# Attention and Fourier filter in one kernel: helper copies of the queries and keys issued one segment later, the last segment's v rows in buffers of their own, and the first feature loads placed behind a stack of queries

## The chip, the cores and the metric

The kernel runs on one core of a Trainium2 chip. The time is the device time of one execution in microseconds (us); three runs of the kernel before took 716.06 to 720.59, median 717.18. One further execution was recorded by the hardware profiler: it took 717.81 us, and the span from its first to its last instruction is 716.1 us. All instruction times below come from that execution and count from the start of the span. TensorE is called PE, VectorE DVE, ScalarE ACT, GpSimd POOL and SyncE SP; SP does no arithmetic, it issues DMAs, in the order of the program, and waits.

## The reference

Two independent computations, whose results stand side by side in the output.

```python
# A: causal attention in 4 segments of 512 rows, 32 heads of 18, with a memory carried between segments
q,k,v = x@wq, x@wk, x@wv
for s in range(4):
    p = softmax(qs @ ks.T * scale + mask);  a_dot = p @ vs
    num = phi(qs) @ M;  den = phi(qs) @ z + 1e-6          # phi(t) = t+1 if t>0 else exp(t)
    outs.append(g * num/den + (1-g) * a_dot)              # g = sigmoid(beta)
    M = M + phi(ks).T @ vs;  z = z + phi(ks).sum(rows)
a = concat(outs) @ wo
# B: a filter in the frequency domain
b = irfft2(rfft2(x) * (w_r + 1j*w_i))
```

x of A is 2048 x 576, x of B 2048 x 576, everything in float32.

## The kernel before, in words

The order of the work is written out by hand. Python generators emit the instructions; each engine then runs its own instructions in the order in which they were emitted, and an instruction waits for the data, and for the buffers, that it needs. The tiles come from rotating pools: a tile with `bufs=2` can be allocated again once the work on its allocation before the last one is over, DMAs that read it included.

There are four stages.

1. **Forward transform of B** (0 to about 75 us).
2. **Projections of A** (about 75 to 277 us, `projections`, L557). For each of the four segments g come nine units `qk_unit` (L472), each 14 products of 128 x 512 for 128 columns of the queries or keys, and four units `v_unit` (L509), each 14 products of 288 columns for either half of 128 rows of v. A queries-and-keys unit splits its result into three bf16 parts and stores them in DRAM as `qkD` (L499). A unit of v copies its result into a tile `vt` (two buffers; POOL fills its constant columns, L519 and L520, ACT copies the rest, L522) and SP stores it in `vD` (L523). For the segments 0 to 2 the features phi(k) are collected in a tile `pk` (one buffer of 128 x 4 x 576) and multiplied with `vt` for the memory (L529); the last segment needs no memory and doesn't allocate `pk`. The units of B's middle part run on DVE and ACT in between.
3. **Inverse transform of B** (about 277 to 355 us, `inverse`, L287) in 16 units u. A unit multiplies its spectrum with a table `civ` (L300, 18 products), splits the result into tiles `T` (ACT L330 and L337, DVE L332 and L338), and two units later multiplies those with a table `itab` (L311, 14 products); ACT and DVE form the output `yout` (L316 to L319, three buffers) and SP stores it (L320). Between its steps runs `prologue` (L965), which does the first ten score units `s1` (L677) of the attention, three steps each, and pops one or two DMAs per step from a list: the loads for the next stacks.
4. **Attention** (355 us to the end, `attention`, L987), a loop over t=0..132 with one unit of the 128 (segment, head) pairs per trip. Trip t does the scores `s1(t+10)` for the row maxima and `s2(t)` (L720) for the exponentials, and the product with v (`pv`, L749) of earlier trips. The heads are worked in 16 stacks n of eight. The stack's queries `Qs` (three buffers) and keys `Ks` (four) are loaded by seven DMAs each (`stack_dmas`, L655): six of 128 KB from `qkD` and one of 96 KB from a second DRAM tensor `reD`. At the first trip of stack n the loop queues the queries of stack n+2, the keys of stack n+3 and the v rows of stack n+2, and pops two per trip; `s1(8(n+2))`, in trip 8n+6, is the first to read the new queries.

The helper tensor `reD` holds rows 16 and 17 of every head (a head has 18 rows, a stack's DMA takes 16). It is filled per segment by `rest` (L547): twelve copies `reD<-qkD` from DRAM to DRAM, 64 rows of 1 KB each, six for the queries and six for the keys. Before the change all twelve are issued on SP in the segment that produced them, six ahead of unit 11 and six ahead of unit 12, that is among the units of v.

`pq_load` (L799) loads one of five tiles of the features phi(q) of a segment: four of 126 x 512 float32 (252 KB) and one of 72 x 512 (144 KB). Those of segment 1 are loaded in the trips 16 to 20, one each, ahead of the stack load of the trip; they are first read by `den` (L805), which is set in at trip 34.

Of the kernel before, what the change touches and what calls it, by code (L numbers as in the profile page):

```python
# [5 lines left out]
F32=mybir.dt.float32; F32R=mybir.dt.float32r  # L6
# [387 lines left out]
class ATT:  # L394
# [114 lines left out]
    def v_unit(s,g,tb,tp,pp):  # L509
        nc=s.nc  # L510
        P=[]
        for hf in range(2):
            ps=pp.tile([128,288],F32,name="pjv",tag="pj")
            yield from s.passes(ps,g,"wv",slice(288*hf,288*hf+288),slice(128*tb,128*tb+128),True)
            P.append(ps)
            yield
        vt=tp.tile([128,622],F32,name="vt")
        vv=vt[:,:608].rearrange("p (h c) -> p h c",c=19)
        nc.gpsimd.memset(vv[:,:,18:19],1.0)  # L519
        nc.gpsimd.memset(vt[:,608:],0.0)  # L520
        for hf in range(2):
            nc.scalar.copy(vv[:,16*hf:16*hf+16,:18],P[hf].rearrange("p (h c) -> p h c",c=18))  # L522
        nc.sync.dma_start(s.vD[g][tb],vt)  # L523
        if g==3: return
        for _ in range(3): yield
        if tb==0: s.pm=[pp.tile([126,3,7,19],F32,name=f"pm{i}",tag="pm") for i in range(2)]
        for t in range(5):
            w=7 if t<4 else 4; r=18*w
            nc.tensor.matmul(s.pm[t//3][:r,t%3,:w].rearrange("p h c -> p (h c)"),s.pk[:,tb,126*t:126*t+r],vt[:,133*t:133*t+19*w],  # L529
                start=tb==0 and t%3==0,stop=tb==3,skip_group_check=True)  # L530
        if tb<3: return
        yield
        n=g+1
        for t in range(5):
            w=7 if t<4 else 4; r=18*w
            m=tp.tile([126,7,19],F32,name="mm")
            nc.vector.tensor_tensor(m[:r,:w],s.pm[t//3][:r,t%3,:w],s.bm[:r,:w],op=OP.mult)
            z=s.zst[n][:r,t,:w]
            for o,h0,h1,c0,c1 in ((0,0,7,0,18),) if t<4 else ((0,0,2,0,18),(36,2,3,0,12),(48,1,2,6,18),(60,2,4,0,18)):
                k=(h1-h0)*(c1-c0)  # L540
                M,N=[x[:r,t,o:o+k].rearrange("p (h c) -> p h c",c=c1-c0) if x is not None else None for x in (s.Mst[n],s.Mst[g])]
                x=m[:r,h0:h1,c0:c1]
                if n==1: nc.gpsimd.tensor_copy(M,x)
                else: nc.gpsimd.tensor_tensor(M,x,N,op=OP.add)
            if n==1: nc.gpsimd.tensor_copy(z,m[:r,:w,18])
            else: nc.gpsimd.tensor_tensor(z,m[:r,:w,18],s.zst[g][:r,t,:w],op=OP.add)
# [10 lines left out]
    def projections(s,xp,tp,pp,wv,pace,hook):  # L557

        live=[]
        s.nid=wv.tile([128,128],BF,name="nid"); s.nc.scalar.activation(s.nid,s.ident,AF.Copy,scale=-1.0)  # L560
        lw=s.load_w("wv",576,wv,xp,288,"xl",4)
        def advance():
            for l in list(live):
                try: next(l)
                except StopIteration: live.remove(l)
        tot=pace.left-12
        for g in range(4):
            if g<3: xq=[s.xprep(g+1,t,(xp,s.x0)[g%2],xp,[128,512],"xst",2) for t in range(5)]
            rest=s.rest(g)
            for i in range(13):  # L570
                for _ in range(6 if i>10 else 0): rest.pop(0)()
                u=s.qk_unit(g,i,tp,pp) if i<9 else s.v_unit(g,i-9,tp,pp)
                if i==4 and g<3: s.pk=tp.tile([128,4,576],F32,name="pk",bufs=1)
                next(u)
                hook(g,i)
                next(lw,None); next(lw,None)
                if g<3 and i in (4,6,8,10,12): next(xq[(i-4)//2])
                if g<3 and i in (1,3,5,7,9): next(xq[(i-1)//2])
                w=tot/(36-18*.3+12*2.7+3*2.0+.2)*((2.7 if g<3 else 2.0 if i<12 else .2) if i>8 else .7 if s.third(g,i) else 1.0)
                advance()  # L580
                pace.take(w*.7)
                advance()
                next(u)
                pace.take(w*.3)
                live.append(u)
        while live: advance()

    def att_setup(s,cp):
# [376 lines left out]
    def prologue(s):  # L965

        nc,io=s.nc,s.io
        yield
        s.masks()
        s.load_v(0)  # L970
        q=s.stack_dmas(1,0)+s.stack_dmas(1,1)+s.stack_dmas(2,0)+s.stack_dmas(2,1)+[lambda: s.load_v(1)]+s.stack_dmas(3,1)
        for i in range(2): yield
        i=0
        for t in range(10):
            for _ in s.s1(t):
                for _ in range(1+(i%5==0)):
                    if q: q.pop(0)()
                i+=1
                yield
            if 2<=t<6: nc.gpsimd.dma_start(s.Ks[t-2][108:110].rearrange("p h c -> p (h c)"),io["neg1"])  # L980
            if t in (3,7): m=s.mpath(t//4); next(m)
            if t in (4,8): next(m); next(m,None)
        assert not q
    def homes(s):

        for n,t,b in (("oh",F32R,5),("ol",F32R,5),("am",F32,5),("pq",F32,5),("ux",F32,3)): s.tp.tile([126 if n in ("am","pq") else 128,512],t,name=n,bufs=b)
    def attention(s,tp,ps):  # L987
        nc=s.nc; s.tp,s.ps,s.psm,s.mtag=tp,ps,s.ps1,"s1"
        s.homes()
        def steps(gen,i):  # L990
            for _ in range(i):
                try: next(gen)
                except StopIteration: return
        m=None
        q=[]
# [12 lines left out]
        for t in range(133):  # L1008
            k,hh=divmod(t,4); n,qd=divmod(k,2); g=k//8
            if t==3: nc.gpsimd.memset(s.cap,3.0e38)  # L1010
            if t==4: nc.gpsimd.affine_select(out=s.cap,in_=s.cap,pattern=[[1,128]],compare_op=OP.is_ge,fill=0.0,base=0,channel_multiplier=-1)
            if hh==0 and qd==0:
                if 0<n<14: q+=s.stack_dmas(n+2,0)
                if 0<n<13: q+=s.stack_dmas(n+3,1)
                if n+2<16: q.append(lambda n=n: s.load_v(n+2))
            st=t%32
            if 16<=t<21: s.pq_load(1,t-16)
            if t==34: bg.insert(0,s.den(1,lane))
            if st==8 and g>0:
                def ln(g=g):  # L1020
                    r=s.recip(s.rD[g-1],s.rrD[g-1],s.g1,False,"rr",2)
                    for i in range(8):
                        next(r)
                        if 2<i<6: s.ux_load(g-1,i-3)
                        yield
                    yield from r
                    bg.append(s.mixed(g))
                    if g<3: bg.append(s.between(g,lane))
                lane.append(ln())
            if t==124: lane.append(s.recip(s.rD[3],s.rrD[3],s.g1,False,"rr"))  # L1030
            if 125<=t<128: s.ux_load(3,t-125)
            a=s.s1(t+10) if t+10<128 else iter(())
            b=s.s2(t) if t<128 else iter(())
            if q: q.pop(0)()
            if qu: qu.pop(0)()
            if hh==(0 if k>29 else 3) and m is not None: steps(m,1)
            steps(a,1)
            steps(b,1)
            r=(t-5)%4
            if r%2: run_bg(1)  # L1040
            steps(a,1)
            steps(b,1)
            if 5<=t<129: s.pv((t-5)//4,(t-5)%4)
            if t==129:
                for j in range(4): s.pv(31,j)
                s.pv_out(31)
                u=s.u_dmas(15)
                rb=s.recip(s.rD[3],s.rrD[0],s.g1,False,"re")
                qu+=[u[0],lambda: next(rb)]+u[1:]
            steps(a,1)  # L1050
            steps(b,1)
            s.free=not bg and t<116
            if hh==(3 if k==29 else 2) and m is not None: steps(m,1)
            if hh==1 and k+2<32: m=s.mpath(k+2); next(m)
            if 7<=t<131 and t%4==3:
                s.pv_out((t-7)//4)
                if t%8==3:
                    u=s.u_dmas((t-11)//8)
                    if t<120: s.later(1,lambda u=u: qu.extend(u))
                    else: qu+=u  # L1060
            for l in list(lane):
                try: next(l)
                except StopIteration: lane.remove(l)
            if q: q.pop(0)()
            if qu: qu.pop(0)()
            run_bg((.3,1,.5,1)[r])
            s.due(t)
# [3 lines left out]
        i=0  # L1071
# [28 lines left out]
        for u in range(8):  # L1100
            tb,hf=divmod(u,2); s.last_proj(u,4,None if u>2 else 1)
# [105 lines left out]
```

## Time and profile before

| | us |
|---|---|
| median of three runs | 717.18 |
| profiled execution | 717.81 |
| its span | 716.1 |
| PE busy | 674.7 (94%) |
| DVE busy | 558.0 (78%) |
| ACT busy | 443.5 (62%) |
| POOL busy | 215.1 (30%) |

A matmul is shown from its start to its modelled end, and matmuls overlap, so a PE that is busy all the time is not at its peak; what counts is where it stands idle and what ended that. A row of the timeline gives start, duration, engine, line, operation, output and inputs, shapes and count, and in brackets the idle time before it with what released it. In a row of stretches stand the length, the busy time of each engine with its count of instructions, the granted share of the PE clock, the mean busy share of the 16 DMA engines (over 1 where packets overlap) and GB/s.

### The profile page before, as it was taken

Reading aid. Unit: us, or ns where it says so; the run is one execution under the profiler, and the core shown is the slowest. Engines: PE = TensorE matmul, PEld = TensorE weight load, DVE = VectorE, ACT = ScalarE, POOL = GpSimd, SP = SyncE. Lnnn points to the kernel's source line nnn. Section 1 sums busy time; section 2 is a strip of 40 time slices with the busy share of each in tenths; the row PEclk is TensorE's granted clock in tenths of the full one; section 3 lists DMA queues with packets and bytes.
Section 4 is the critical chain, followed back from the end, with each engine's and each line's share of the span. In section 5 each row is a group of like instructions: output and inputs, shape, how many; then the busy total and the mean of one; then the engine's idle time right before and its main releaser. Section 6 shows DMA issues by size and latency. Waiting matters only on the chain.

```text
span 716.1 us, 14217 instructions
## 1 busy us (share of the span) xinstructions
PE 674.7 (94%) x4829; PEld 496.4 (69%) x4829; DVE 558.0 (78%) x1237; ACT 443.5 (62%) x999; POOL 215.1 (30%) x422
## 2 busy tenths in 40 slices
PE   4999999999999998999989699998999999999997
PEld 4999779889779788999844354444566445564677
DVE  5999999899989886698588587987656876568353
ACT  3667795583584562444378477776766777667741
POOL 2110000100200211365156553543424564245210
PEclk9999999999999999899999899999999999999999
DMA  9877446555664778999639987979768988552232
GB/s 339 269 230 205 149 141 210 198 186 167 207 204 139 215 219 278 196 230 224 169 91 190 167 161 146 188 151 167 134 148 166 166 156 156 130 139 67 87 101 81
DMA packets 89321, 124.73 MB, mean 174 GB/s; under 512 B 13994, under 2 KB 56600, under 8 KB 89112
## 3 DMA queue, kind: packets, MB, share of 16 engines
q1 hardware_dynamic: 82656, 107.78, 61.4%
q0 software_dynamic: 6592, 16.04, 8.9%
q8 instruction: 38, 0.62, 0.4%
q14 instruction: 35, 0.29, 0.2%
HBM read 85.45 MB, written 41.39 MB: 177 GB/s over the span
## 4 chain that ended last, share of the span: by engine, by line
PE 65%; DVE 11%; DMA 10%; ACT 8%; issue 4%; POOL 1%; SPq 0%; ACTq 0%; DVEq 0%; POOLq 0%
PE pv L758 9%; PE pj L469 7%; PE po L919 6%; PE pjv L469 5%; PE s L684 5%; PE i L300 4%; PE i L311 4%; PE s L692 4%; PE s L728 3%; PE s L732 2%; DMA vD<-vt 2%; PE po L951 2%; DMA Qs<-qkD 2%; PE pm L529 2%; DMA xin<-xb 2%
## 5 line engine op out<-in xcount | busy, mean ns | idle before, releaser
L688 DVE CUSTOM_DVE_ANT_0 junk<-s,mask 128x512 bf16<-128x512 f32 (+1 forms) x256 | 141.5, 553 | 54.1 <-PE s L684 42.1
L694 DVE TENSOR_REDUCE mx<-s 128x4 f32<-128x512 f32 x128 | 87.8, 686 | 23.7 <-PE s L693 22.4
L729 ACT ACTIVATE P<-s 128x512 f32<-128x512 f32 x128 | 77.2, 603 | 26.5 <-PE s L728 24.7
L734 ACT ACTIVATE P<-s 128x512 f32<-128x512 f32 x128 | 76.9, 601 | 8.7 <-PE s L733 5.0
L758 PE MATMUL pv<-P,vs 128*32 128x512 f32 (+3 forms) x1024 | 82.1, 439 | 0.0
L738 ACT ACTIVATE P<-s 128x256 f32<-128x256 f32 x128 | 49.4, 386 | 47.8 <-PE s L737 47.7
L741 POOL TENSOR_SCALAR_AFFINE_SELECT P<-P 128x512 f32<-128x512 f32 x116 | 69.6, 640 | 4.1 <-ACT P L729 3.4
L758 PEld LDWEIGHTS pv<-P,vs 128*32 128x32 f32 x1024 | 26.7, 109 | 45.0 <-issue 41.5
L469 PE MATMUL pj<-x,wqkh 128*128 128x512 f32 x162 | 55.9, 406 | 0.0
L519 POOL MEMSET vt<- 128x32 f32 x16 | 2.4, 162 | 155.2 <-PE pm L529 110.8
L210 DVE TENSOR_TENSOR t<-Z 128x580 f32<-128x580 f32 x64 | 46.4, 755 | 0.1
L210 DVE TENSOR_TENSOR Z<-t 128x580 f32<-128x580 f32 x64 | 45.8, 753 | 0.0
L300 PE MATMUL i<-civ,Y 128*128 128x256 f32 (+1 forms) x288 | 39.7, 293 | 3.3 <-DVE T L332 3.3
L684 PE MATMUL s<-Ks,Qs 108*128 108x512 bf16 (+1 forms) x128 | 42.1, 329 | 0.0
L493 ACT CAST sp<-pj 128x512 bf16<-128x512 f32 x36 | 21.1, 585 | 31.9 <-DVE pj L489 31.9
L142 PE MATMUL f<-ftab,eh 128*128 128x290 f32 (+1 forms) x160 | 31.0, 312 | 10.0 <-DMA ftab<-ftab 10.0
L300 PEld LDWEIGHTS i<-civ,Y 128*128 128x128 f32 (+1 forms) x288 | 37.5, 189 | 3.5 <-DVE T L332 3.5
L311 PE MATMUL i<-itab,T 128*128 128x290 f32 (+1 forms) x224 | 37.1, 316 | 0.1
L469 PEld LDWEIGHTS pj<-x,wqkh 128*128 128x128 f32 x162 | 30.4, 188 | 8.7 <-issue 2.0
L469 PE MATMUL pj<-xh,wqkl 128*128 128x512 f32 x90 | 35.6, 395 | 0.0
L469 PE MATMUL pj<-x,wqkl 128*128 128x512 f32 x90 | 35.6, 395 | 0.0
L469 PE MATMUL pj<-xh,wqkh 128*128 128x512 f32 x90 | 35.5, 395 | 0.0
(227 smaller groups left out, 1833.0 us busy)
## 6 DMA issues: line engine op xcount, KB each, us to landing
qkD<-sp SPq DMA_DIRECT2D x36, 384.0 KB
Ks<-qkD SPq DMA_DIRECT2D x72, 128.0 KB
x<-qkD SPq DMA_DIRECT2D x60, 128.0 KB
Qs<-qkD SPq DMA_DIRECT2D x60, 128.0 KB
xin<-xb SPq DMA_DIRECT2D x16, 384.0 KB
cfw<-cfw POOLq DMA_DIRECT2D x16, 384.0 KB, 4.4
civ<-civ POOLq DMA_DIRECT2D x16, 384.0 KB, 6.3
vs<-vD SPq DMA_DIRECT2D x16, 330.0 KB
```

The source lines that it names most:

```text
L210: v.tensor_tensor(o,a,b,op=op)
L300: nc.tensor.matmul(p[:m,k],Y[i][:,q,c*128:c*128+m],cc[:,hl,o:o+256],start=n==0,stop=n==5)
L311: nc.tensor.matmul(p,x,t,start=n==0,stop=n==6)
L469: s.nc.tensor.matmul(out,a,b,start=i==0,stop=i==len(L)-1)
L684: nc.tensor.matmul(out,Q[:108,h,128*i:128*i+128],K[:108,h,:128*(i+1)],start=True,stop=True)
L688: nc.vector.tensor_tensor_reduce(out=junk[:,:w],in0=src,in1=s.mask[:,512-w:],scale=1.0,scalar=-3.0e38, op0=OP.add,op1=OP.max,accum_out=s.m ...
L694: nc.vector.tensor_reduce(out=s.mx[k][:,hh],in_=pa.rearrange("p (b c) -> p b c",c=128),axis=mybir.AxisListType.X,op=OP.max)
L729: nc.scalar.activation(P[0][:,hh],p0,AF.Exp,scale=SC)
L734: nc.scalar.activation(P[1][:,hh],p1,AF.Exp,scale=SC)
L738: nc.scalar.activation(P[2][:,hh],p2,AF.Exp,scale=SC)
L741: if k<29: nc.gpsimd.affine_select(out=x,in_=x,pattern=pat+[[1,128]],compare_op=OP.is_ge,fill=0.0,base=0,channel_multiplier=-1)
L758: nc.tensor.matmul(s.pvt[32*hh:32*hh+32,128*j:],vt[:,j,19*h:19*h+32],mv[0][:,hh,mv[1]],start=j==0,stop=j==2,skip_group_check=True)
```

## The change

Three edits, all in the order of work and in buffers; the arithmetic stays.

- **Copies.** `s.left=s.rest(g)` keeps the twelve copies of segment g until the next segment, where two each are issued ahead of the units 2 to 7. The last segment's twelve are issued in the prologue, one at every second step, behind the stack loads of that step.
- **Buffers of v.** In the last segment the units 0 to 2 of v write slices of a fresh `pk` tile, 622 columns each, and only unit 3 takes a `vt` buffer.
- **Features.** The five loads of segment 1's phi(q) go from the trips 16 to 20 to the trips 19 to 23.

```diff
@@ v_unit
-        vt=tp.tile([128,622],F32,name="vt")
+        if g==3 and tb==0: s.pk=tp.tile([128,4,576],F32,name="pk",bufs=1).rearrange("p a b -> p (a b)")
+        vt=s.pk[:,622*tb:622*tb+622] if g==3 and tb<3 else tp.tile([128,622],F32,name="vt")
@@ projections
-            rest=s.rest(g)
             for i in range(13):
-                for _ in range(6 if i>10 else 0): rest.pop(0)()
+                if g>0 and 1<i<8:
+                    for _ in range(2): s.left.pop(0)()
...
                 live.append(u)
+            s.left=s.rest(g)
         while live: advance()
@@ prologue
                 for _ in range(1+(i%5==0)):
                     if q: q.pop(0)()
+                if i%2 and s.left: s.left.pop(0)()
                 i+=1
                 yield
...
-        assert not q
+        assert not q and not s.left
@@ attention
-            if 16<=t<21: s.pq_load(1,t-16)
+            if 19<=t<24: s.pq_load(1,t-19)
```

## The prediction

> **What bounds the kernel now.** I read the page first, then the stretches of each stage, then PE's waits in them, and then the chain of waits and the rows of each engine around the two places where PE stands still.
>
> ```profile
> PE 674.7 (94%) x4829; PEld 496.4 (69%) x4829; DVE 558.0 (78%) x1237; ACT 443.5 (62%) x999; POOL 215.1 (30%) x422
> ```
>
> PE is busy 94% of the span; what can be won lies in the idle 41 us and in work done at a lower clock. The stretches, in the columns explained above:
>
> ```profile
> 75.00:128.00 53.00, 51.64 (x295) 43.59 (x294) 51.01 (x83) 37.36 (x83) 0.34 (x4) 1.00 0.53 169
> 286.00:300.00 14.00, 14.00 (x95) 13.53 (x93) 7.66 (x17) 6.41 (x16) 4.87 (x7) 0.81 0.82 187
> 300.00:350.00 50.00, 50.00 (x396) 47.72 (x395) 42.31 (x101) 22.48 (x55) 26.28 (x39) 1.00 1.18 226
> 386.00:412.00 26.00, 19.77 (x160) 9.25 (x159) 15.43 (x47) 14.09 (x34) 15.07 (x22) 0.87 0.92 180
> ```
>
> The inverse transform (300 to 350) is full on PE and full on the DMA engines at once, 1.18. Behind 286, PE has a clock of only 0.81. In 386 to 412 it is idle for 6.2 us and has 0.87, with the DMA engines at 0.92. The longest waits of PE in 75 to 277, 277 to 300 and 360 to 716 are:
>
> ```profile
> PE pj L497 <- ACT sp L493: 3.0, 4, 0.9
> PE i L300 <- DVE T L332: 3.3, 1, 3.3
> PE s L692 <- DMA pq<-pqD: 5.8, 1, 5.8
> ```
>
> The projections lose 3.0 us in four waits, none of them on v or on the copies: what the change does to the segments 0 to 2 is off PE's path. The other two waits are the places the change touches.
>
> **The first place: end of the projections.** The chain of waits and the rows of PE, ACT, DVE and SP:
>
> ```profile
> 266.93 8.40 DMA vD<-vt
> 275.40 4.42 DMA vD<-vt
> 281.19 2.88 DMA vD<-vt
> 289.22 2.82 PE i L311 x14
> 292.04 2.15 PE i L300 x18
> 341.44 1.90 PE i L311 x14
> ```
>
> ```profile
> 277.28 4.43 PE L300 MATMUL i<-civ,Y 128*128 128x256 f32 x36
> 285.01 4.21 PE L300 MATMUL i<-civ,Y 128*128 128x256 f32 x18 [3.30 <-DVE T L332]
> 275.42 0.71 ACT L522 COPY vt<-pjv 128x288 f32<-128x288 f32 x2 [4.05 <-DMA vD<-vt]
> 279.92 0.70 ACT L522 COPY vt<-pjv 128x288 f32<-128x288 f32 x2 [3.79 <-DMA vD<-vt]
> 280.50 0.60 ACT L330 CAST T<-i 128x512 fp32r<-128x512 f32 x1
> 281.24 1.04 ACT L284 CAST Y<-Z 128x512 fp32r<-128x512 f32 x2
> 282.19 0.58 ACT L330 CAST T<-i 128x512 fp32r<-128x512 f32 x1
> 284.27 0.69 DVE L332 TENSOR_TENSOR T<-i,T 128x512 fp32r<-128x512 f32 x1 [1.98 <-POOL Y L285]
> 270.99 3.80 SPq L555 DMA_DIRECT2D reD<-qkD  x6
> 277.20 3.88 SPq L555 DMA_DIRECT2D reD<-qkD  x6
> ```
>
> Two groups of six copies hold SP for 3.80 and 3.88 us, each ahead of a store of v (275.40 and 281.19). ACT waits 4.05 and 3.79 us for `vt` buffers that those stores empty, so the splits of the inverse's first units (280.50, 282.19) come late. DVE's split at 284.27 starts 0.2 us after the third store lands (281.19+2.88=284.07); POOL, named there, is not what the chain follows. I read it as a T tile that lies where that `vt` buffer was. PE, done with 36 products at 281.71, waits to 285.01, and then does 18 products in 4.21 us and 14 in 2.82, for which it later takes 2.15 and 1.90.
>
> *After.* The three slices need no store to land; unit 3 takes a buffer that segment 2 left. The one wait that is added, for the old `pk`, ends with segment 2's sums, which PE does before any product of segment 3's v. ACT's copies follow their products, which end as the 36 begin, and its first split follows 12 of the 36 products: 277.28+12x0.123=278.8 (0.123 is 4.43/36). It lasts 0.60, the small split after it about 0.4 (an estimate: fewer columns), the casts 1.04: ACT is free at 281.0, just when the second unit's first twelve products (the 30th of 36, 280.97) are done. Split to 281.7, DVE 0.69 to 282.4: PE goes on at 282.5 instead of 285.01, 2.5 us sooner. The last store of v, issued at about 278.2, behind ACT's 0.70, with nothing ahead of it on SP, lands by 281.1 at the 2.88 of its neighbour, ahead of DVE. POOL's fills of `vt`, queued behind the same stores, go early too; its next work follows ACT's casts. PE's idle time is then 0.8 us, no more than its waits of 0.9 in the projections, whose stretches show a clock of 1.00, so the slow products go too: 4.21-2.15=2.06 and 2.82-1.90=0.92. Sum: 2.5+2.06+0.92=**5.5 us**. What is late next is PE itself; the stretch from 300 on has not a tenth idle. Bounds: 2.5 if the clock falls all the same, 6.3 if no gap is left.
>
> **The copies, where they go.** In segments 1 to 3: twelve issues each at 3.80/6=0.63 us, two per unit, ahead of that unit's stores on SP. They wait for nothing (their source landed a segment ago), and the DMA engines have room there (0.53). They delay stores by up to 1.3 us; that reaches PE only through buffers two or three units deep. Zero, and if that cover were gone 1.3 us less per unit.
>
> In the prologue they are not free: twelve DMAs of 64 KB are 768 KB, at 226 GB/s (221 KB/us) **3.5 us** of DMA time in a stage that has none left. SP, late, then holds back the stores of `yout`:
>
> ```profile
> 337.89 0.36 SPq L320 DMA_DIRECT2D yb<-yout  x1
> 347.46 0.46 DVE L318 TENSOR_TENSOR yout<-E,i 128x290 f32<-128x290 f32 x1 [0.89 <-ACT E L316]
> 391.47 8.38 DMA Qs<-qkD
> ```
>
> Three buffers: the store issued at 337.89 must land before DVE's 347.46, 9.57 us later; transfers that queue take 8.4 (391.47 and, above, 266.93). So 1.2 us are to spare, and 3.5-1.2=2.3 us reach DVE. DVE has 15% idle time there and PE reads two units behind it, so I put 0.5 us on PE; bounds 0 and 2.3.
>
> **The second place: trip 22.** SP's rows, a wait of SP in 386 to 412, and PE's rows:
>
> ```profile
> 389.59 0.49 SPq L803 DMA_DIRECT2D pq<-pqD  x1
> ...
> 394.64 2.27 SPq L668 DMA_DIRECT2D Qs<-qkD  x2
> 397.06 0.33 SPq L803 DMA_DIRECT2D pq<-pqD  x1
> 397.83 0.30 SPq L668 DMA_DIRECT2D Qs<-reD  x1
> SPq L668 <- DMA vs<-vD: 1.3, 1, 1.3
> ```
>
> ```profile
> 394.69 1.28 PE L758 MATMUL pv<-P,vs 128*32 128x384 f32 x16
> 398.55 1.30 PE L758 MATMUL pv<-P,vs 128*32 128x512 f32 x16
> 399.90 0.27 PE L737 MATMUL s<-Qs,Ks 110*128 110x256 bf16 x1
> 405.99 0.58 PE L692 MATMUL s<-x,Qs 108*128 108x384 bf16 x2 [5.82 <-DMA pq<-pqD]
> 410.45 0.93 PE L758 MATMUL pv<-P,vs 128*32 128x384 f32 x8
> 423.90 0.38 PE L692 MATMUL s<-Ks,Qs 108*128 108x384 bf16 x2
> ```
>
> Two trips take 398.55-394.69=3.86 us; the pair with the wait takes 410.45-398.55=11.90, so 8.0 are lost: 5.8 idle, 2.0 in products at a lower clock (0.58 for L692, else 0.38). PE's wait is for stack 4's queries, whose seventh load is issued at 397.83. Four feature loads (first 389.59, fourth 397.06) go ahead of it through the same queue; SP is the only queue that they are moved in, past the six loads of Qs. SP's wait says that the v load before them landed at 394.6. From there to 405.9 came 4x252+6x128+96=1872 KB, 166 KB/us; the stretch has 180 GB/s (176 KB/us). I take 170.
>
> *After*, one feature load is ahead: 252+768+96=1116 KB, 6.6 us: the queries land at 401.2. PE wants them at 400.2 (399.90+0.27). **1.0 us** of wait instead of 5.8.
>
> But the DMA engines were full, and the loads moved back now stand ahead of stack 5's queries, which trip 30 wants. Before, trip 30 began at 423.90. After, it is due eight trips, 4x3.9=15.6 us, past 401.2: 416.8. Behind 401.2 must land stack 5's keys 864, features 3x252+144=900, v 330 (128x4x165 floats), four stores of U 288 (36 rows of 2 KB each) and stack 5's queries 864: 3246 KB, 19.1 us: **420.3**. So PE waits there for 3.5 us, and the gain at trip 30 is 423.9-420.3=3.6 of the 8.0. Bounds, by 158 (5% under what was measured) and 176 KB/us: 1.7 and 4.5. Both waits over 3 us (3.30 and 5.82) were followed by a lowered clock that cost 2 to 3 us; I charge 2.0 here. **1.6 us** stay. Past trip 30 no features are left in the way: stack 6 has a full 15.6 us.
>
> **The sum.** 5.5-0.5+1.6=6.6 us off the profiled 717.81: 711.2. The median of the runs is 0.6 below that execution, so 710.6.
>
> **The rivals.**
> *The clock holds at trip 30* (the wait is 3.5 us, hardly longer than the 3.30 that lost it): 2.0 more, 708.6. [...]
> *No second wait*: transfers speed up when the features no longer stand in front, and all 8.0 stay: 717.2-13.0=704.2. Against it: 0.92 to 1.18 wherever loads queue.
> *The copies hold up the inverse by the whole 2.3 us and a little clock*: 713.
> *The slices are not kept apart*: if the program waits per tile, each v unit waits for the store before it, 4 us as now, and the first 5.5 are gone: 716. Against: `Qs` and `Ks` of stack 0 also share one tile and are loaded and read independently.
> *Slower: the twelve copies cost a turn in the queue instead of bytes.* The prologue's transfers take 8.4 us with eight under way, 1.05 us a turn. Twelve turns are 12.6 us; less 1.2 to spare and about 2 of PE's distance to DVE, PE stands 9.4 us: 717.2-5.5+9.4-1.6=719.5. It decides from (5.5+1.6+3.2)/12=0.86 us a copy; 768 KB at the measured rate give 0.29. Nothing shows a small copy costing a whole turn: SP issued six in 3.80.
>
> **How the numbers follow.** Forecast 0.42, clock holds 0.22, no second wait 0.10, inverse held up 0.12, slices 0.08, slower 0.06. The likeliest is 710.6. The range 705.0 to 715.5 leaves out half of "no second wait", the slices and the slower case, and takes in both rates of the second place and the 2.3 of the copies. One per cent, about what a measurement of this kernel tells from no change, is 7.2 us: faster means below 710.0. That is a third of the forecast, most of "clock holds" and all of "no second wait": 0.42. Within: 0.54. Slower by over 1% (above 724.4) needs the slower case to be worse than priced: 0.04.
>
> **What would show it.** First place: no wait of ACT for vD at 270 to 280, PE's wait for DVE L332 under 1.5 us, clock 1.00 behind it. Prologue: DVE L318 waiting for yb, or not. Second place: PE's wait at trip 22 about 1 us, a new wait of L692 for a Qs load eight trips later of 2 to 5 us, and whether the clock drops there. Wrong would be: a wait of over 3 us inside the inverse, or no wait at trip 30.

## The result and the profile after

| | before | after |
|---|---|---|
| median, same chip, us | 718.22 (714.70 to 722.11, 13 runs) | 713.49 (708.35 to 715.77, 13 runs) |
| profiled execution, us | 717.81 | 712.57 |
| its span, us | 716.1 | 710.8 |

The ratio of after to before is 0.9923, with a 95% interval of 0.9899 to 0.9948: 0.8% faster, 4.7 us by the medians and 5.2 us by the profiled executions. That is within 1%, and between the two bounds of the predicted range; the forecast was 710.6.

The page's line of busy times, and three of the stretches that were shown of before (286 to 300, 300 to 350, 386 to 412), in the changed kernel:

```profile
PE 673.3 (95%) x4829; PEld 494.5 (70%) x4829; DVE 558.2 (79%) x1237; ACT 444.2 (62%) x999; POOL 215.2 (30%) x422
```

```profile
286.00:300.00 14.00, 14.00 (x112) 13.22 (x111) 11.75 (x27) 6.96 (x18) 7.50 (x10) 1.00 1.03 204
300.00:350.00 50.00, 49.95 (x390) 47.51 (x390) 39.62 (x95) 21.17 (x52) 23.27 (x36) 1.00 0.97 228
386.00:412.00 26.00, 23.21 (x195) 11.25 (x188) 18.24 (x56) 16.99 (x43) 15.37 (x24) 0.93 1.01 173
```

Behind 286 the clock is 1.00 where it was 0.81, and 112 matmuls fit where 95 did. In 386 to 412 PE is idle for 2.8 us instead of 6.2, at 0.93 instead of 0.87. Lines of the attention have moved down by two: L692 is now L694, L668 is L670.

The first place, in the rows of PE, ACT and SP of the changed kernel (start, duration, and in brackets the idle time before the row):

```profile
282.33 2.39 PE L300 MATMUL i<-civ,Y 128*128 128x256 f32 x18 [0.76 <-DVE T L332]
284.56 2.05 PE L311 MATMUL i<-itab,T 128*128 128x290 f32 x14
...
341.78 2.31 PE L300 MATMUL i<-civ,Y 128*128 128x256 f32 x18
```

```profile
279.20 0.59 ACT L330 CAST T<-i 128x512 fp32r<-128x512 f32 x1 [1.44 <-DMA vD<-pk]
```

```profile
277.82 0.32 SPq L524 DMA_DIRECT2D vD<-vt  x1
```

PE stands 0.76 us where it stood 3.30, and the 18 and 14 products behind it take 2.39 and 2.05 us where they took 4.21 and 2.82. The last store of v is issued at 277.82; before, the last two went out one behind the other from 281.19 on. At the end of the inverse PE's last 18 products with `civ` start at 341.78; before, the same row stood at

```profile
347.20 2.31 PE L300 MATMUL i<-civ,Y 128*128 128x256 f32 x18
```

so the whole stage came 5.42 us earlier. One wait is new: ACT's first split stands 1.44 us for the store out of a slice of `pk`.

The attention, in the rows of PE around its three longest waits between 355 and 716:

```profile
394.50 0.27 PE L739 MATMUL s<-Qs,Ks 110*128 110x256 bf16 x1
397.45 0.38 PE L694 MATMUL s<-x,Qs 108*128 108x384 bf16 x2 [2.68 <-DMA Ks<-qkD]
...
416.94 0.38 PE L694 MATMUL s<-Ks,Qs 108*128 108x384 bf16 x2 [2.00 <-DMA Ks<-qkD]
...
492.70 0.39 PE L694 MATMUL s<-Ks,x 108*128 108x384 bf16 x2 [1.66 <-DMA x<-reD]
498.39 0.38 PE L694 MATMUL s<-Ks,x 108*128 108x384 bf16 x2
```

The rows of L694 are the trips 22, 30, 62 and 64. (The transfer named as a releaser is the one that landed last by then; what the first two rows read is `Qs`.) Before, they began at 405.99, 423.90 (both shown), and

```profile
499.49 0.39 PE L692 MATMUL s<-Ks,x 108*128 108x384 bf16 x2 [1.49 <-DMA x<-reD]
...
503.93 0.38 PE L692 MATMUL s<-Ks,x 108*128 108x384 bf16 x2
```

The gain over before is thus 5.42 us at the end of the inverse, 8.54 at trip 22 (405.99-397.45), 6.96 at trip 30, 6.79 at trip 62, 5.54 at trip 64, and 5.3 at the end of the span. The wait at trip 22 fell from 5.82 to 2.68, one of 2.00 appeared at trip 30, and 1.25 us were lost between trip 62 and trip 64, where the wait is hardly longer than before (1.66 against 1.49).

The granted clock says what happened there. From 20 us on, but for the last 2 us, it falls in the trace of before to 0.50 at 284.37 and 403.84, 35 times 3.413 us apart, each time for 6.83 us; in the trace of after at 398.37 and 493.94, 28 times 3.413 us apart, each time for 3.41. So I cut the time into steps of 3.41 us that end at these instants. In the changed kernel, two steps at trip 22, two at trip 30, two at trip 62 (length, PE busy, ..., and the granted clock third from the end):

```profile
394.96:398.36 3.40, 0.91 (x6) 0.58 (x7) 0.57 (x4) 0.49 (x3) 1.77 (x3) 1.00 0.98 164
398.37:401.78 3.41, 3.41 (x21) 1.62 (x22) 2.77 (x8) 2.55 (x6) 1.25 (x2) 0.50 0.88 197
...
415.44:418.84 3.40, 1.90 (x14) 1.27 (x15) 1.30 (x3) 1.16 (x4) 0.42 (x2) 1.00 0.92 133
418.86:422.26 3.40, 3.40 (x32) 1.72 (x31) 2.94 (x9) 2.48 (x7) 2.78 (x5) 1.00 0.65 169
490.53:493.94 3.41, 1.75 (x19) 0.93 (x12) 1.21 (x5) 0.95 (x3) 0.42 (x2) 1.00 0.93 180
493.95:497.35 3.40, 3.40 (x19) 1.32 (x20) 2.88 (x8) 3.34 (x9) 1.45 (x2) 0.50 0.66 167
```

PE was idle for 2.49 us of the first step (73%), and the clock of the next is half. At trip 30 it was idle for 1.50 us of a step (44%), and the clock held. At trip 62 it was idle for 1.66 us of 3.41 (49%), and the next step ran at half clock.

### The profile page after: what moved, and what is told of

Its sections match the earlier page's. It is cut to its first block, busy times and chain, and to the rows that moved or that the text cites. A ratio compares the mean times of both kernels' runs of the same rounds, so it can differ in the third digit from the quotient of the medians.

```text
span 710.8 us, 14215 instructions
## 1 busy us (share of the span) xinstructions
PE 673.3 (95%) x4829; PEld 494.5 (70%) x4829; DVE 558.2 (79%) x1237; ACT 444.2 (62%) x999; POOL 215.2 (30%) x422
## 4 chain that ended last, share of the span: by engine, by line
PE 55%; DVE 12%; ACT 7%; DMA 7%; issue 4%; POOL 1%; SPq 0%; DVEq 0%; ACTq 0%; POOLq 0%
PE pv L760 9%; PE po L921 6%; PE s L686 5%; PE pjv L469 5%; PE i L300 4%; PE i L311 4%; PE s L694 4%; PE pj L469 3%; PE s L730 3%; PE s L734 2%; PE po L953 2%; DVE pj L489 2%; DMA Ks<-qkD 2%; PE s L695 2%; DVE junk L690 2%
## 5 line engine op out<-in xcount | busy, mean ns | idle before, releaser
L300 PE MATMUL i<-civ,Y 128*128 128x256 f32 (+1 forms) x288 | 37.9, 284 | 0.8 <-DVE T L332 0.8
L300 PEld LDWEIGHTS i<-civ,Y 128*128 128x128 f32 (+1 forms) x288 | 35.8, 181 | 1.0 <-DVE T L332 1.0
```

Of the source, the lines that this page charges most:

```text
L300: nc.tensor.matmul(p[:m,k],Y[i][:,q,c*128:c*128+m],cc[:,hl,o:o+256],start=n==0,stop=n==5)
```

## The experiments

The theory behind them: the copies among the units of v and the v buffers together made the first wait, and the features are worth the rest. The rivals: one of the two alone made it; the features give nothing in sum; the copies cost time where they went. Each was run beside the kernel before on the same chip: the first four rows on one chip, where the kernel before had a median of 719.16 us, the last four on another, with 719.25. Rows of different chips are compared by their ratios. The diffs are against the changed kernel, except where the text says otherwise.

| kernel | median, us (runs) | ratio to before, 95% interval |
|---|---|---|
| features back at the trips 16 to 20 | 714.55 (9) | 0.9926, 0.9897 to 0.9955 |
| copies back among the units of v | 719.65 (10) | 1.0003, 0.9972 to 1.0035 |
| two `vt` buffers as before | 712.00 (4) | 0.9891, 0.9847 to 0.9936 |
| features at the trips 0 to 4 | 706.86 (4) | 0.9822, 0.9779 to 0.9866 |
| prologue's copies issued twice | 712.98 (10) | 0.9917, 0.9890 to 0.9945 |
| features at 0 to 4 and two `vt` buffers | 707.50 (6) | 0.9839, 0.9808 to 0.9871 |
| copies moved for the last segment only | 714.61 (10) | 0.9938, 0.9911 to 0.9965 |
| features at 0 to 4, two `vt`, loads of wo later | 708.07 (6) | 0.9846, 0.9809 to 0.9883 |

**Features back.**

```diff
-            if 19<=t<24: s.pq_load(1,t-19)
+            if 16<=t<21: s.pq_load(1,t-16)
```

> The changed kernel with the five feature loads back in the trips 16 to 20. Theory (the two places are independent; 5.4 us come from the end of the projections, the net of the second place is 1.5): PE resumes the inverse at 282.3, trip 22 waits 5 to 6 us again with the lowered clock behind it, no wait at trip 30, and the time lies 1.5 us above the changed kernel and 5.4 below the kernel before. Rival (the feature loads are nearly the whole gain): the time goes back to that of the kernel before. Rival (their place is worth nothing): the time equals the changed kernel's and trip 22 waits no more than 2.7.

PE's longest wait in the attention, and the stretches around it:

```profile
PE s L694 <- DMA pq<-pqD: 8.6, 1, 8.6
```

```profile
394.02:397.43 3.41, 1.55 (x18) 0.35 (x18) 1.64 (x6) 1.29 (x4) 2.46 (x6) 1.00 1.01 168
397.44:400.84 3.40, 0.00 (x0) 0.00 (x0) 0.00 (x0) 0.00 (x0) 0.63 (x1) 1.00 1.03 160
400.86:407.67 6.81, 3.50 (x15) 1.95 (x16) 2.04 (x6) 1.60 (x4) 0.09 (x1) 0.50 0.74 143
```

With the features in their old place, PE, which now comes to trip 22 about 5 us earlier, waits 8.6 us there instead of 5.8: the loads do not come earlier by as much as PE does, so trip 22 takes back part of what the first place gives. The DMA engines are busy all through the wait (1.03). There is no wait at trip 30. In the profiled executions the move of the features is worth 2.0 us (714.58 against 712.57). The ratios, 0.9926 and 0.9923, show nothing; the half widths of their intervals, 0.0029 and 0.0025, leave some 0.4% (3 us) either way. So the move gives little in time, and how much is not settled; in the kernel of the next experiment, which has the move without the gain of the first place, it even costs 1.0 us up to trip 30 in the profiled execution (that trip begins at 426.09 against 423.90 before, while the inverse ends 1.22 late).

**Copies back.**

```diff
+            rest=s.rest(g); s.left=[]
             for i in range(13):
-                if g>0 and 1<i<8:
-                    for _ in range(2): s.left.pop(0)()
+                for _ in range(6 if i>10 else 0): rest.pop(0)()
...
-            s.left=s.rest(g)
```

> The changed kernel with the twelve copies of each segment issued among the units of v again, six ahead of unit 11 and six ahead of unit 12. Theory (copies hold SP, and the store of v behind them holds a T tile): ACT no longer waits for vD, the last store of v is issued at about 280 instead of 277.8 and lands at 282.5 to 284, DVE's second split waits for it, PE resumes at 283.3 to 285.0, and 2 to 5 of the 5.4 us are lost. Rival (the buffers alone do it): PE resumes at 282.3 and the time equals the changed kernel's.

ACT's row, PE's, SP's, the chain of waits, and a stretch at the begin of PE's wait (used in the last section), each of this kernel:

```profile
284.55 0.59 ACT L330 CAST T<-i 128x512 fp32r<-128x512 f32 x1 [6.27 <-DMA vD<-pk]
```

```profile
287.63 3.73 PE L300 MATMUL i<-civ,Y 128*128 128x256 f32 x18 [5.53 <-DVE T L332]
```

```profile
277.38 4.01 SPq L556 DMA_DIRECT2D reD<-qkD  x6
```

```profile
281.50 2.87 DMA vD<-pk
...
284.55 0.59 ACT T L330
```

```profile
280.43:283.83 3.40, 1.67 (x15) 1.44 (x13) 0.00 (x0) 0.00 (x0) 0.00 (x0) 1.00 0.62 214
```

The whole gain is gone (1.0003), and at the first place this kernel is worse than before: 5.53 us of waiting instead of 3.30. The six copies hold SP from 277.38 to 281.4, the store of a slice, issued behind them, lands at 284.37 (281.50+2.87), and only then may ACT write its first T. The own buffers free ACT's copies of v, but not what comes next, because T lies where a slice of `pk` lies (I infer the place from this wait).

**Two buffers of v.**

```diff
-        if g==3 and tb==0: s.pk=tp.tile([128,4,576],F32,name="pk",bufs=1).rearrange("p a b -> p (a b)")
-        vt=s.pk[:,622*tb:622*tb+622] if g==3 and tb<3 else tp.tile([128,622],F32,name="vt")
+        vt=tp.tile([128,622],F32,name="vt")
```

> The changed kernel with the two rotating vt buffers of v in the last segment, copies and features as changed. Theory (the moved copies do nearly all): the first store lands at 275.1, the second, issued at 271, at 278.5, so ACT waits about 1 us for each of the two, PE resumes the inverse at 282.7, 0.4 us later than the changed kernel, and the time is within 0.5 us of it. Rival (the buffers do it): ACT waits 3 to 4 us per store again, PE resumes at 284 to 285 and 3 to 5 us are lost.

ACT's rows and PE's:

```profile
274.85 0.70 ACT L522 COPY vt<-pjv 128x288 f32<-128x288 f32 x2 [3.59 <-DMA vD<-vt]
278.51 0.70 ACT L522 COPY vt<-pjv 128x288 f32<-128x288 f32 x2 [2.96 <-DMA vD<-vt]
279.10 0.60 ACT L330 CAST T<-i 128x512 fp32r<-128x512 f32 x1
```

```profile
282.34 2.40 PE L300 MATMUL i<-civ,Y 128*128 128x256 f32 x18 [0.76 <-DVE T L332]
```

ACT waits for the two buffers nearly as long as before, 3.59 and 2.96 us (4.05 and 3.79 before), and it costs nothing: its first split starts at 279.10, a tenth of a microsecond earlier than with the slices, and PE resumes after the same 0.76 us at the same time. What is left of the wait is PE's own order: in this trace the chain of work goes from the 30th of the 36 products, done at 280.9, over ACT's second split at 280.92 to DVE's at 281.60.

Before, the copies held back two stores, and each cost something. The one issued at 275.40 (270.94 here) freed a buffer for ACT's last copies of v, so ACT's splits came 1.3 to 1.4 us later than here (280.50 and 282.19 against 279.10 and 280.92). The one issued at 281.19 held DVE's split for some 1.4 us more (284.27, though ACT's second split was over at 282.77). So moving the copies ends the first wait by itself, and the buffers give nothing that shows. The interval of the ratio overlaps that of the changed kernel.

**Copies of the last segment only.**

```diff
+            s.left=s.rest(g)
             for i in range(13):
-                if g>0 and 1<i<8:
-                    for _ in range(2): s.left.pop(0)()
+                for _ in range(6 if g<3 and i>10 else 0): s.left.pop(0)()
...
-            s.left=s.rest(g)
```

> The changed kernel with the copies of the segments 0 to 2 issued where they were before, among their own segment's units of v, and only the last segment's in the prologue. If the gain of the first place comes from the last segment's copies alone and the copies of the segments 0 to 2 are off PE's path, as the prediction has it (cost and gain zero): the same as the changed kernel, 713 to 714 us, PE's units of the inverse 5.4 us early, waits in the projections as before (3.0 us in sum within 0.5). If the copies of the segments 0 to 2 held back the projections where no wait of PE showed it: slower by what PE loses between 75 and 277 us, 1 to 3 us.

PE's waits in 75 to 277 (in total, times, longest), a wait of ACT in 260 to 300, and PE's row at the first place:

```profile
PE pj L497 <- ACT sp L493: 3.0, 4, 0.9
ACT T L330 <- DMA vD<-pk: 2.2, 1, 2.2
```

```profile
283.84 1.34 PE L300 MATMUL i<-civ,Y 128*128 128x256 f32 x9 [1.50 <-DVE T L332]
```

The waits in the projections are 3.0 us, as in both kernels; the ratio, 0.9938, has an interval that overlaps the changed kernel's over most of its length. Where the copies of the segments 0 to 2 stand makes no difference that these runs can tell; the twelve of the last segment do it all.

The gap at the first place was 1.50 us in this execution and 0.76 in the changed kernel. It follows ACT's wait for the store out of a slice of `pk`, which was 1.44 us in the changed kernel and 2.2 here. In the kernels with features back, features at 0 to 4 and copies issued twice, which have the slices too, that wait was 2.30, 1.84 and 2.13 us, and PE's gap 1.57, 1.12 and 1.40: beyond 1.44 us the wait reaches PE almost one to one. The three kernels with two `vt` buffers, where ACT's splits wait for no store, have gaps of 0.76, 0.76 and 0.86. So the slices cost up to 0.8 us where their store lands late. Why it lands later in one execution than in another is not shown.

**Copies issued twice.** The prologue's twelve copies are each followed by a second one into a tensor that nobody reads.

```diff
-                if i%2 and s.left: s.left.pop(0)()
+                if i%2 and s.left:
+                    s.left.pop(0)()
+                    s.twin.pop(0)()
```

> The changed kernel, with the prologue's twelve copies issued a second time behind each of them, into a spare tensor that nobody reads (twelve more DMAs of 64 KB, 768 KB more). Theory A (copies of 64 KB fit between the other transfers of that stage, and cost PE nothing as long as the stores of yout land in time): the inverse's units start as early over the kernel before as in the changed kernel (5.4 us from unit 4 on), and at most 0.5 us are lost by trip 10; trip 22's wait may grow by up to 1 us, since the loads of the first stacks are late. Theory B (the stage is full, 221 KB/us, and only the slack of 1.2 us at yout hid the first twelve, which took 3.5 us of DMA time at that rate): the second twelve come out in full, 3.5 us of PE waiting in the inverse or at the first scores. Theory C (a copy costs a turn in the queue, 1.05 us, as in the prediction's slower case): 12 us of waiting.

The stretches of the inverse, and PE's row at its begin and that of its last 18 products with `civ`:

```profile
286.00:300.00 14.00, 14.00 (x112) 13.31 (x111) 11.45 (x25) 7.35 (x19) 6.83 (x9) 1.00 0.98 233
300.00:350.00 50.00, 49.98 (x392) 47.67 (x391) 40.35 (x98) 21.54 (x54) 24.24 (x36) 1.00 0.99 244
```

```profile
283.54 2.41 PE L300 MATMUL i<-civ,Y 128*128 128x256 f32 x18 [1.40 <-DVE T L332]
...
343.00 2.31 PE L300 MATMUL i<-civ,Y 128*128 128x256 f32 x18
```

Twelve more copies cost PE nothing in the stage: it is never idle from 286 to 350, and the 1.2 us by which it is behind the changed kernel at the end (343.00 against 341.78) were there at the start, 0.6 of them the longer first wait (ACT waited 2.13 us for the store out of a slice). Behind the stage, the wait at trip 22 is 2.99 us, against 2.68 in the changed kernel. The stage that I called full moved 244 GB/s instead of the 226 of before. Theory A holds; a full stage (B) and a turn in the queue for each copy (C) are both refuted, B by 3.5 us and C by 12.

**Features at the trips 0 to 4.**

```diff
-            if 19<=t<24: s.pq_load(1,t-19)
+            if t<5: s.pq_load(1,t)
```

> The changed kernel with the five feature loads in the trips 0 to 4, where the DMA engines are a quarter busy. Theory (the waits at the trips 22 and 30 are 1.15 MB of features ahead of stack loads in a full queue, and only their place decides): no wait at trip 30, at most 0.5 us at trip 22, clock 1.00 from 277 to the wait of trip 62, and the time is 5 to 6.5 us below the changed kernel. Rival (the transfers are the bound whatever their order): waits at the trips 22 and 30 of 4 us or more in sum, and no more than 1.5 us gained.

PE's row at trip 22:

```profile
398.21 0.38 PE L694 MATMUL s<-x,Qs 108*128 108x384 bf16 x2 [1.97 <-DMA Ks<-qkD]
```

There is no wait at trip 30, the granted clock of the whole execution is 1.000, and the time is 706.86: faster than the changed kernel, with intervals that don't meet. The loads went into a stretch that had been empty: from 356 to 365 the DMA engines were busy for 4% in the changed kernel and for 80% here. The wait at trip 22 is still 1.97 us, with no feature ahead of the queries; at most 0.5 was expected.

**Features at the trips 0 to 4 and two buffers of v.** Both edits above, together.

> The changed kernel with the features in the trips 0 to 4 and the two vt buffers of before, both of which were tried alone. If the buffers of v give nothing and the place of the features the rest, as those two runs read: the same time as with the features alone, 706 to 708 us (ratio 0.982 to 0.986), the inverse 4 to 5.4 us early, one wait of about 2 us at trip 22 and none at trip 30. If the own buffers of v do bring something that the single run hid: 2 to 3 us more, 709 to 710.

PE's row at trip 22 (lines are one lower in number here):

```profile
396.39 0.38 PE L693 MATMUL s<-x,Qs 108*128 108x384 bf16 x2 [1.03 <-DMA uD<-U]
```

The same time as with the features alone (0.9839 against 0.9822, overlapping), so the buffers give nothing here either; the wait at trip 22 is 1.03 us, half of what was expected. These two are the best versions found, 1.6 to 1.8% faster than before.

**Loads of wo later.** With the two edits above, the last four of the six loads of the output weight wait for trip 24.

```diff
             if t>1: yield
+            while t==2 and s.now<24: yield
```

> Features in the trips 0 to 4, two vt buffers, and the last four of the six loads of the output weight wo (295 KB each, 1180 KB) held until trip 24. The wait of 2.0 us that was left at trip 22 with the features at the trips 0 to 4 came from somewhere else. Theory A (whatever bytes are ahead of stack 4's queries decide): with 1180 KB less between 365 and 385 us, at 170 KB/us 6.9 us of transfers, the wait at trip 22 is gone (under 0.3 us), the gain at trip 24 grows by 2 us, and the time falls to 704 to 706 unless trip 30 or trip 62 now waits. Theory B (the wait comes from when SP may issue: the loads of the stacks start only when the score units of the prologue free their tiles, and the queue behind them holds eight): the wait stays at 1.5 to 2 us, time as with the features alone. Rival C (the loads moved behind trip 24 delay stack 5's queries as the features did): trip 30 waits 2 to 4 us, and nothing is won.

PE's row at its longest wait in the attention, and the stretches around trip 22 and around that wait:

```profile
461.39 0.38 PE L884 MATMUL pb<-rr,sel 96*126 96x512 bf16 x1 [2.12 <-DMA rr<-rrD]
```

```profile
386.00:412.00 26.00, 25.89 (x225) 13.08 (x224) 22.72 (x72) 20.96 (x52) 12.54 (x25) 1.00 0.98 164
...
458.71:462.11 3.40, 1.28 (x15) 0.73 (x8) 0.73 (x3) 0.86 (x2) 1.69 (x3) 1.00 1.14 155
462.13:465.53 3.40, 3.23 (x12) 1.56 (x11) 3.18 (x8) 1.97 (x4) 0.00 (x0) 0.50 1.00 175
```

Theory A names the rest of trip 22's wait rightly: with those bytes out of the way PE is busy for 25.89 of 26.00 us. But the time is the same (708.07). Against the kernel without this edit, PE lost the gain again between 424 and 462: it was idle for 1.6 us more from 424 to 440, then came a wait of 2.12 us near trip 50 for `rr`, followed by a step at half clock. That the work which was held back made these waits is argued, not shown. What was lost lay further on than trip 30, where no rival on record had put it.

## Why the prediction was right, and where not

- **First place: 5.5 us predicted, 5.42 measured.** The parts were 2.5, 2.06 and 0.92; PE resumed at 282.33 (predicted 282.5), 2.68 us sooner, and the rest, 2.74, came behind that, 1.82 and 0.77 of it in the 18 and 14 products, now at full clock. That the clock would hold behind a gap of 0.8 us was right too: the gap was 0.76 us, and the clock from 282 to 300 was 1.00. The cause that I named was half wrong: I gave the three slices a part in it. The experiment with two `vt` buffers shows that they have none. With the copies away, the stores that free the rotating buffers land early enough that PE doesn't feel ACT's waits for them, and the wait for the 30th of the 36 products is what remains, as predicted. I also read the two groups of copies as holding back the stores that ACT waited for; the first of those two waits (4.05 us) was for the store issued at 266.93, ahead of all copies. The sentence "The three slices need no store to land" was wrong: ACT's first split waits 1.44 us for one, and where it waited longer, in four other kernels, PE's gap grew to 1.12 to 1.57 us.
- **Copies in the segments 1 to 3: zero.** Right, as far as these runs can tell: with or without the move the waits in the projections are 3.0 us.
- **Copies in the prologue: 0.5 us, bounds 0 and 2.3. Measured 0.** The step that failed is "twelve DMAs are 3.5 us of DMA time in a stage that has none left". I took a busy share of 1.18 for a limit; twelve copies fit, and twelve more after them. PE was busy for 49.95 of the 50 us from 300 to 350.
- **Trip 22: 1.0 us predicted, 2.68 measured.** The terms that were mis-sized are the rate and the start. I let the loads come earlier by as much as PE. PE wanted the queries at 394.77 (394.50+0.27), 5.4 us earlier than the 400.2 of before; the seventh load was issued at 390.12 and PE went on at 397.45, which is 402.9 in the time of before instead of 401.2. The start: the seventh load went out when the v load ahead of it had landed (SP waits 1.8 us for `vs`, issued at 382.94, the eighth DMA before it), which was at 390.1, 4.5 us earlier than the 394.6 of before and not 5.4. The rate: the 1116 KB behind it took until 397.4, 7.3 us at 153 KB/us instead of 6.6 at 170. What held the loads up was not tried on this kernel; the wo experiment, with the features at 0 to 4, points at bytes queued earlier in the attention.

```profile
390.12 0.30 SPq L670 DMA_DIRECT2D Qs<-reD  x1
```

- **Trip 30: a new wait of 3.5 us predicted, 2.00 measured.** The wait is there, and without the move (features back, or at 0 to 4) it is not: the mechanism is right. It was over-sized by what trip 22 and the slow step behind it had already taken: in the time of before, PE was due at 420.4 (416.94-2.00+5.42), 3.6 later than predicted, and went on at 422.4, 2.1 later than predicted. Where PE lost still more at trip 22 (copies issued twice: 2.99 us and two slow steps) there was no wait at trip 30 at all.
- **The lowered clock, 2.0 us, charged at trip 30.** It fell at trip 22 and held at trip 30, so the rival "the clock holds at trip 30" (its chance, 0.22, was my estimate) was right as to its event and wrong as to the time: 708.6 was not reached, since the cost had come eight trips before. The net of the second place, 6.96-5.42=1.54 us, is the predicted 1.6 by errors that cancel, which is luck.
- **What was missed: trip 62.** 1.25 us went to a clock that fell behind a wait of 1.66 us, where before 1.49 us left it alone. The wait there is not tied to the change: among the kernels whose attention is the same as the changed one's, PE waits 2.83 us at trip 62 with the copies moved for the last segment only, and at most 0.23 us with two `vt` buffers or copies issued twice. Another 0.2 us went between trip 64 and the end (5.54 to 5.3). From the predicted 6.6 to the measured 5.3 (716.1-710.8) it goes: -0.08 at the first place, +0.5 in the prologue, -0.06 in the second place, -0.17 from trip 30 to trip 62, -1.25 there, -0.24 behind it.
- **What would show it.** The sign named for the first place, no wait of ACT for `vD` at 270 to 280, failed by the 1.44 us that end at 279.20, and PE did not feel them. The slower rival (a turn in the queue for each copy) is refuted by PE's full stretch from 300 to 350 and by the doubled copies; its 8.4 us had been read at 266.93 and 391.47, ahead of that stage and behind it. "No second wait" is refuted by trip 30.
- **One per cent.** The measured 0.8% lies in the case to which the forecast gave most.

## What to carry to other kernels

When a queue issues several DMAs ahead of a store, ask whose memory that store frees, and follow that one wait: here the copies ahead of the last stores were everything at the first place, and buffers that took away 6.5 us of visible waiting of ACT (3.59+2.96) gave nothing, and cost up to 0.8 us where their own store landed late. A stage that comes earlier can make its consumer wait longer for loads that do not come earlier with it (8.6 us at trip 22 instead of 5.8, with the features in their old place), so follow a gain on to the next load that ends late. Loads wanted later can go far ahead instead of just behind the urgent ones: the same five loads at the trips 0 to 4, where the DMA engines had been nearly idle, gave another 1%, with no second wait.

## What the runs showed of the hardware

The granted clock fell after waits much shorter than I had reckoned with (1.66 us at trip 62), and not by their length. The rows above and these two of the kernel with two `vt` buffers, at trip 22 and trip 30, show it:

```profile
392.69:396.10 3.41, 2.12 (x22) 0.58 (x20) 2.15 (x8) 1.86 (x6) 2.47 (x7) 1.00 1.00 172
396.11:399.51 3.40, 2.36 (x17) 1.46 (x17) 1.62 (x4) 1.61 (x5) 1.20 (x1) 1.00 0.97 219
...
413.17:416.57 3.40, 1.04 (x8) 0.69 (x9) 0.89 (x4) 0.77 (x3) 0.42 (x2) 1.00 0.86 165
416.58:419.99 3.41, 3.41 (x20) 1.56 (x21) 2.58 (x8) 2.37 (x6) 1.43 (x3) 0.50 0.71 177
```

Both waits are 2.3 to 2.4 us. The first is spread over two of the steps of 3.41 us, 1.29 and 1.04 us, and the clock held; the second lies in one step, 2.36 us, and the clock fell. Over the whole traces of before and after, from 20 us on and but for the last microseconds, the clock fell from 1.00 behind steps in which PE was idle for 49, 73, 78 and 100%, and held at 1.00 behind all others, of 44% or less. In single steps of the other kernels it fell behind 62% (loads of wo later, 458.71 to 462.11) and 69% (two `vt` buffers, 413.17 to 416.57), and held behind 46% (copies of the last segment only, 396.10 to 399.48: 1.56 us of 3.38). Two steps, of 51% (copies back, 280.43 to 283.83: 1.73 of 3.40) and 55% (features back, 394.02 to 397.43: 1.86 of 3.41), held all the same, and the clock fell only behind the wholly idle step that followed. So in these traces the lowest idle share with a fall behind it is 49% and the highest without one is 55%: the idle share alone doesn't settle it. The falls at 284.37 before and at 398.37 after lie 33.4 steps apart, so in these two executions the steps don't begin with the span. That the place of the steps against the waits is a part of the scatter between runs of one kernel (708 to 716 us for the changed one) is argued from this, not shown: only one execution of each kernel was traced.
